# Linear attention and an MLP on one core: token groups of 864 for six of eight batches, d_ff in quarters, and a sign taken by Prelu

## The chip, the core and the metric

The kernel runs on one NeuronCore of a Trainium2 chip. The core has a matrix engine (TensorE, PE in the profile), a vector engine (VectorE, DVE), an activation engine (ScalarE, ACT), a general engine (GpSimd, POOL) and a queue engine (SyncE, SP) that starts most DMA transfers. Each works through its own list of instructions in order and waits on semaphores for the others. Matmul results land in PSUM, eight banks of 512 fp32 columns; everything else on the chip lies in SBUF. The metric is device microseconds of one launch.

## What is computed

```python
def phi(x):                                   # 8 batches, 8 heads, 576 tokens, head_dim 64; 128 features
    proj = np.einsum('bhsd,md->bhsm', x, omega)
    h = proj - np.sum(x * x, axis=-1, keepdims=True) / 2.0
    h = h - np.max(h, axis=-1, keepdims=True)
    return np.exp(h) / np.sqrt(m)
q_p, k_p = phi(q * scale), phi(k * scale)
kv = np.einsum('bhsm,bhsd->bhmd', k_p, v); z = np.sum(k_p, axis=2)
num = np.einsum('bhsm,bhmd->bhsd', q_p, kv)
den = np.einsum('bhsm,bhm->bhs', q_p, z)[..., None] + 1e-06
x = (num / den) as 4608 tokens x 512          # 8 batches x 576 tokens
h = x @ w_in                                  # 512 x 2048
g = h * erf(np.maximum(h, 0.0) + np.log1p(np.exp(-np.abs(h))))
out = g @ w_out                               # 2048 x 512
```

The weights w_in and w_out come as float64.

## The kernel before, in words

`build` records every step as an operation with the engines that may run it, an estimate of its duration on each, the tiles that it reads and writes, and for some a date (`plan`). `Plan.order` then walks through time, gives each free engine the operation with the nearest due time whose tiles have a slot, and writes one list of instructions. The engines' order is fixed by that list. `SLOTS` has the slots of each pool, `CAPS` how many of them one stream may hold.

**Attention** works in pairs of heads, four pairs (n = 4b to 4b + 3) per batch. `project` makes 128 features for 9 chunks of 128 rows in three PSUM banks (ppq, ppk), DVE takes the maxima (mxq, mxk), ACT the exponentials (fq, fk), `key_values` makes kvp, `turn` transposes the query features (pt, qh, ql), and `attend` makes numerator and denominator (nd) in two spans of 384 and 192 columns for each head (`SPANS`); ACT inverts the denominator through Ln and Exp (rc), DVE multiplies (xs). Pairs from the ninth on split their operands into a high and a low fp32r part, three matmuls for one product; the first eight run in plain fp32.

**The MoE** works batch by batch, 576 tokens as two tiles of T = 288 columns. The hidden dimension goes in two halves (`ph`), each of four d_ff tiles (`f`, 256 columns of d_ff). `split` makes high and low parts of x and of its sums (xh, xl). The first product is plain (`plain1`, banks h, eight products) for batches 0 to 2 and Winograd's form of Strassen's scheme (`gemm1`, banks hX, hY, hZ, seven products) for batches 3 to 7; each product is two contraction steps of three matmuls. `chain` takes two d_ff tiles: softplus on ACT (gs from hs), erf on ACT, the gate (hs from gs), the high part (gh) and the rest (gl). The second product (`gemm2`, blocks `e` 0 to 3 of 128 output columns, two banks o each) runs half a d_ff behind the first: `BLOCKS` sets the order f0 f1, e0, f2, e1, f3, e2, e3, where e belongs to the half before. Its banks are copied to `os` after the first half and added after the second, and stored.

**The weights** of float64 are turned into fp32 once, in 32 units of 512 KB, during batches 0 and 1: `w_load` brings the words, ACT shifts the exponent (`w_bias`), DVE shifts (`w_shift`), puts the sign in (`w_sign`) and the low word's bits (`w_tail`), then ACT makes the high part (`w_high`) and DVE the rest (`w_rest`). The finished unit is stored to DRAM (wdw) and fetched from there ever after. In batch 2 the sums for the Winograd form are made (`make_sums`, tiles R, S, cS).

What sets the order around the change: the dates of the matmuls (`at`), which start from `starts`, one entry for each half of a batch, and the dates of the pairs (`pair_time`), which spread each batch's four pairs over the batch before. Draining operations have no date of their own; theirs follows from what needs them next.

Of the kernel before, what the change touches and what calls it, by code (L numbers as in the profile page):

```python
# [329 lines left out]
def build(emit):  # L330
# [3 lines left out]
    seq = [(b, ph) for b in range(B) for ph in range(NPH)]  # L334
    starts = [START0]
    for b, ph in seq:
        starts.append(starts[-1] + FP * (STEP2 + (STEP1 if b >= PLAIN else STEP1 * 8 / 7))
                      + (NP * PAIR / 2 if b + 1 < B else 0.0))

    def begin(b):  # L340
        return starts[2 * b]

    def pair_time(n, x):
        b, p = divmod(n, NP)
        if b == 0:
# [1 line left out]
        each = (begin(b) - begin(b - 1)) / NP
        return begin(b) - LEAD - (NP - p) * each + x * each * 1.2
# [28 lines left out]
    def make(u, t):  # L377

        nm = "_".join(str(c) for c in u)
        st = pl.tile("gl", f"st{nm}", [P, HW, 2], I32, "st")  # L380
# [13 lines left out]
    def room():  # L394
        count[0] += 1
        return SLOTS["w"] - CAPS["cv"] if clock[0] < starts[2 * PLAIN + 1] else None
# [769 lines left out]
```

## Time and profile before

| | us |
|---|---|
| median of three timed runs | 1075.67 |
| their range | 1073.88 to 1076.56 |
| the profiled execution | 1073.78 |
| its span, first to last instruction | 1072.0 |

The granted TensorE clock is 0.998 of full speed over the span. The span has 21687 instructions. A row of the profile gives an engine, what it writes from what (names of tiles, buffer numbers left out), the form and the count, then busy time, the mean of one in ns, and the idle time before it with what ended it. A matmul's duration is modelled and overlaps the next one's, so a stream of matmuls is read from start to start. L824 is the line of a helper that records all of them.

### The profile page before, as it was taken

The page shows a single profiled execution, that of the slowest core. Times are in us where ns is not written, and L with a number is a line of the kernel's source. Part 1 is how long each engine was busy: PE and PEld are TensorE (multiplying, and loading weights), DVE is VectorE, ACT ScalarE, POOL GpSimd, SP SyncE. Part 2 cuts the span into 40 slices and gives each one's busy share as a digit, 9 for nine tenths or more (in the row PEclk, how much of TensorE's full clock was granted, in tenths as well). Part 3 has the DMA queues.
Part 4 walks back from the last instruction along what each step waited for, and adds up shares of the span by engine and source line. Part 5 has one row for each costly group of instructions (what it writes and reads, how often), then busy time and mean ns, then how long its engine had stood idle before and what let it go on. Part 6 is the DMA issues. An engine that isn't in the chain of part 4 may idle for free.

```text
span 1072.0 us, 21687 instructions
## 1 busy us (share of the span) xinstructions
PE 1051.2 (98%) x8272; PEld 1025.9 (96%) x8272; DVE 734.6 (69%) x1316; ACT 719.4 (67%) x1390; POOL 352.1 (33%) x306
## 2 busy tenths in 40 slices
PE   7899899999999999999999999999999999999998
PEld 7798899999999999999999999999999999999998
DVE  4889988877488586965768566766658656564431
ACT  7878878875668565867657666775667765564540
POOL 6222104100066294812334312522127222263330
PEclk9999999999999999999999999999999999999999
DMA  8376568776557777587776767768675775668771
GB/s 229 119 239 223 204 235 269 251 256 203 201 197 262 251 260 265 172 279 260 256 238 217 259 231 254 253 210 278 229 252 188 278 234 204 205 204 295 264 244 47
DMA packets 97382, 247.02 MB, mean 230 GB/s; under 512 B 10976, under 2 KB 11360, under 8 KB 97280
## 3 DMA queue, kind: packets, MB, share of 16 engines
q1 hardware_dynamic: 97216, 245.57, 67.9%
q8 instruction: 66, 1.08, 0.4%
q14 instruction: 36, 0.29, 0.1%
q0 software_dynamic: 64, 0.07, 0.0%
HBM read 210.99 MB, written 34.60 MB: 229 GB/s over the span
## 4 chain that ended last, share of the span: by engine, by line
PE 92%; DMA 3%; DVE 3%; ACT 1%; issue 1%; SPq 0%; POOL 0%; DVEq 0%; POOLq 0%; ACTq 0%
PE o L824 37%; PE h L824 13%; PE hX L824 12%; PE hY L824 6%; PE kvp L824 5%; PE nd L824 5%; PE ppq L824 4%; PE ppk L824 4%; PE hZ L824 3%; PE pt L824 2%; DMA st<-w 1%; DVE wt L824 1%; DMA uq<-qN 1%; DMA w<-wdw 1%; DVE xs L824 0%
## 5 line engine op out<-in xcount | busy, mean ns | idle before, releaser
L824 PE MATMUL o<-gh,w 128*128 128x288 f32 x2048 | 445.2, 298 | 0.2 <-ACT fq L824 0.2
L824 PEld LDWEIGHTS o<-gh,w 128*128 128x128 f32 x2048 | 339.3, 188 | 2.3 <-ACT fq L824 0.5
L824 PE MATMUL o<-gl,w 128*128 128x288 f32 x1024 | 301.7, 295 | 0.0
L824 PEld LDWEIGHTS o<-gl,w 128*128 128x128 f32 x1024 | 192.6, 188 | 0.0
L824 PE MATMUL h<-xh,w 128*128 128x288 f32 x768 | 174.6, 303 | 6.3 <-DVE w L824 2.8
L824 PE MATMUL hX<-xh,wb 128*128 128x288 f32 x640 | 162.0, 299 | 0.0
L824 PEld LDWEIGHTS h<-xh,w 128*128 128x128 f32 x768 | 129.7, 190 | 9.3 <-DVE w L824 4.5
L824 ACT ACT_TABLE_LOAD x92 | 118.0, 1283 | 2.3 <-PEq L1157 0.7
L824 PE MATMUL h<-xl,w 128*128 128x288 f32 x384 | 113.9, 297 | 0.0
L824 PEld LDWEIGHTS hX<-xh,wb 128*128 128x128 f32 x640 | 113.5, 188 | 0.4
L824 POOL TENSOR_TENSOR uk<-uk 128x288 f32<-128x288 f32 (+1 forms) x54 | 49.4, 934 | 181.4 <-DMA uk<-kN 119.9
L824 POOL TENSOR_TENSOR uq<-uq 128x288 f32<-128x288 f32 (+1 forms) x46 | 42.4, 942 | 184.5 <-DMA uq<-qN 66.1
L824 POOL TENSOR_TENSOR gl<-hs,gh 128x576 fp32r<-128x576 f32 x50 | 89.4, 1809 | 39.7 <-ACT gh L824 29.4
L824 PE MATMUL hX<-xl,wb 128*128 128x288 f32 x320 | 94.6, 296 | 0.0
L824 DVE TENSOR_REDUCE mxk<-ppk 128x4 f32<-128x512 f32 (+2 forms) x96 | 50.7, 553 | 62.1 <-PE ppk L824 61.1
L824 POOL TENSOR_TENSOR hs<-gs,hs 128x576 f32<-128x576 f32 x26 | 42.9, 1669 | 149.5 <-ACT gs L824 149.5
L824 DVE TENSOR_TENSOR hs<-gs,hs 128x1152 f32<-128x1152 f32 x51 | 81.2, 1600 | 13.4 <-ACT gs L824 13.4
L824 ACT ACTIVATE hs<-hX 128x288 f32<-128x288 f32 x75 | 30.8, 410 | 85.8 <-PE hX L824 82.9
L824 ACT ACTIVATE fq<-ppq,mxq 128x128 f32<-128x128 f32 x288 | 78.6, 386 | 13.5 <-DVE mxq L824 13.2
L824 ACT ACTIVATE rc<-nd,eps 64x192 f32<-64x192 f32 (+1 forms) x128 | 63.6, 497 | 33.3 <-PE nd L824 30.7
L824 ACT ACTIVATE fk<-ppk,mxk 128x128 f32<-128x128 f32 x288 | 79.9, 385 | 3.8 <-DVE mxk L824 3.3
L824 PE MATMUL hY<-xh,wb 128*128 128x288 f32 x320 | 81.3, 299 | 0.0
(106 smaller groups left out, 2115.9 us busy)
## 6 DMA issues: line engine op xcount, KB each, us to landing
w<-wdw SPq DMA_DIRECT2D x144, 512.0 KB, 4.9
wb<-wdcS SPq DMA_DIRECT2D x160, 256.0 KB, 4.1
wb<-wdw SPq DMA_DIRECT2D x120, 256.0 KB, 3.9
st<-w SPq DMA_DIRECT2D x32, 512.0 KB, 5.1
wdw<-w SPq DMA_DIRECT2D x32, 512.0 KB, 3.7
v<-vP SPq DMA_DIRECT2D x32, 325.0 KB, 4.3
out<-os SPq DMA_DIRECT2D x32, 288.0 KB, 3.6
wdcS<-cS SPq DMA_DIRECT2D x16, 512.0 KB, 5.1
```

The costliest lines, as they stand in the source:

```text
L824: return tc.keep_in_program_order(method(*args, **kwargs))
```

## The change

**Token groups.** `SUPERS` puts groups in place of batches: two of 2 x 288 tokens and four of 2 x 432. Groups 0 to 2 are plain, 3 to 5 Winograd. `FROM` has where each begins, `pieces` maps a span of a batch to the tiles of the groups, `need` has the last batch that a group needs: 0, 1, 3, 4, 6, 7. So the pairs of two batches fall into group 1's time and into group 3's. The sums for the Winograd form are made in group 2 (`SUMS`).

**Quarters.** d_ff goes in four parts of two tiles (`NQ`, `GP`). In each the two tiles' products are merged, then come the four blocks e of the part before. Each block takes one unit of w_out and 24 matmuls. Its two banks are copied to `os` in the first part and added in the other three.

**Pools.** hs, gs, gh, gl and what attention borrows from them share one pool "g" of ten slots; staging, R and S share the pool "w" with the weights. Blocks o may hold three PSUM banks in place of two.

**Dates.** Drains of h, hX, hY, hZ and o are due `DRAIN` = 2 us behind their last matmul, the divisions get a date from `DIVIDE`, and the planner's estimates of matmuls, drains and DMA issues follow the tile's width.

**Smaller parts.** `SPANS` becomes 288 and 288. ACT's `w_bias` is a Prelu whose slope gives negative numbers their sign bit, and `w_sign` goes. The maxima of the pairs from the ninth on stay in the middle PSUM bank until they are shifted. Omega is loaded from ACT's queue in place of POOL's. The output is one array of 512 x 4608. `less` and `exponential_all` are not used, since `LESS` is empty.

```diff
-T = 288
+SUPERS = ((288, True), (288, True), (432, True), (432, False), (432, False), (432, False))
+FROM = tuple(2 * sum(t for t, _ in SUPERS[:i]) for i in range(len(SUPERS) + 1))
+SUMS = max(i for i, (_, plain) in enumerate(SUPERS) if plain)
+NG = NPH * FP
+GP = 2
+NQ = NG // GP
...
-SLOTS = dict(w=8, u=3, f=2, mx=3, sq=3, v=2, qh=1, ql=1, kh=1, kl=1, xs=4, xh=2, xl=2,
-             hs=4, gs=2, gh=6, gl=6, os=4, ps=8)
-CAPS = dict(st=2, wt=2, wp=2, cv=2, att=4, moe1=5, moe2=2)
+SLOTS = dict(w=8, g=10, u=2, f=2, mx=3, sq=3, v=2, qh=1, ql=1, kh=1, kl=1, xs=10, xh=2, xl=2,
+             os=4, ps=8)
+CAPS = dict(st=2, wt=1, wp=2, cv=2, att=4, moe1=5, moe2=3, hs=4, gs=2, w=6)
...
-SPANS = ((0, 384), (384, 192))
-BLOCKS = ((("f", 0), ("f", 1)), (("e", 0),), (("f", 2),), (("e", 1),), (("f", 3),), (("e", 2),), (("e", 3),))
+SPANS = ((0, 288), (288, 288))
+DRAIN = 2.0
+DIVIDE = 4.0
...
+    need = [max(b for b in range(B) if FROM[i] < (b + 1) * S and b * S < FROM[i + 1])
+            for i in range(len(SUPERS))]
+    step = [3 * mm(t) * (8 if plain else 7) * KH for t, plain in SUPERS]
+    per = [NG * step[i] + NQ * KT * 2 * GP * 2 * 3 * mm(SUPERS[i][0]) for i in range(len(SUPERS))]
+    more = [(need[i + 1] - need[i]) * NP if i + 1 < len(SUPERS) else 0 for i in range(len(SUPERS))]
...
-        pl.op("psign", [("V", 0.68, -1e9)], lambda e: E.w_sign(st, w), reads=[(st, 0), (w, 0)],
-              writes=[(w, 0)])
...
-            pl.op("hout", [("A", 0.42, -1e9), ("V", 0.46, 0.0)],
-                  lambda e: E.h_out(e, hs.ap[:, i, t, :], hp), reads=[(hp, 0)], writes=[(hs, (i, t))])
+            pl.op("hout", [("A", d["A"], -1e9), ("V", d["V"], 0.0)],
+                  lambda e: E.h_out(e, hs.ap[:, i, t, :], hp, T), reads=[(hp, 0)], writes=[(hs, (i, t))],
+                  plan=clock[0] + DRAIN)
...
+            for block in (("f", 0), ("e", 0), ("e", 1), ("e", 2), ("e", 3)):
+                what, x = block
                 if what == "f":
-                    lists.append((plain1 if b < PLAIN else gemm1)(b, ph, x))
+                    gs = range(GP * q, GP * q + GP)
+                    merged([(plain1 if plain else gemm1)(b, *divmod(g, FP)) for g in gs])
+                    chain(b, gs)
                 elif last:
-                    lists.append(gemm2(*last, x))
+                    merged([gemm2(*last, x)])
...
-    pool.dma_start(om[D:P], omT)
-    pool.dma_start(om[0:D], omT)
+    act.dma_start(om[D:P], omT)
+    act.dma_start(om[0:D], omT)
...
         def w_bias(self, e, t, w):
-            dst, src = w.ap.bitcast(F32), t.ap[:, :, 1].bitcast(F32)
-            if e == "A":
-                act.activation(dst, src, AF.Copy, scale=2.0 ** -112)
...
+            act.activation(w.ap.bitcast(F32), t.ap[:, :, 1].bitcast(F32), AF.Prelu, scale=2.0 ** -112,
+                           alpha=-2.0 ** 32)
...
-        def shift(self, mx, sq):
-            for x in (-half_sq, half_sq):
-                dve.scalar_tensor_tensor(mx.ap, sq.ap, x, mx.ap, op0=ALU.mult, op1=ALU.add)
+        def shift(self, mx, raw, sq):
+            for dst, x in ((raw, -half_sq), (mx.ap, half_sq)):
+                dve.scalar_tensor_tensor(dst, sq.ap, x, raw, op0=ALU.mult, op1=ALU.add)
```

On DVE, while batch 0's first product runs, unit 5 of w_in is unpacked; wt1_0_5 is its PSUM tile, w1_0_5 the finished unit. Before:

```order
L824 TENSOR_SCALAR wt1_0_5_775<-wt1_0_5_775 128x512
L824 SCALAR_TENSOR_TENSOR wt1_0_5_775<-st1_0_5_716,wt1_0_5_775 128x512
L824 TENSOR_REDUCE mxk_1_1_746<-ppk_1_1_2_791 128x3
L824 COPY qh_1_0_812<-pt_1_0_1_800 128x384
L824 COPY qh_1_0_812<-pt_1_0_2_808 128x384
L824 SCALAR_TENSOR_TENSOR wt1_0_5_775<-st1_0_5_716,wt1_0_5_775 128x512
L824 TENSOR_SCALAR wt1_0_6_828<-wt1_0_6_828 128x512
L824 TENSOR_TENSOR w1_0_5_6_717<-wt1_0_5_775,w1_0_5_6_717 128x2x256
```

and now:

```order
L874 TENSOR_SCALAR wt1_0_5_776<-wt1_0_5_776 128x512
L874 SCALAR_TENSOR_TENSOR wt1_0_5_776<-st1_0_5_706,wt1_0_5_776 128x512
L874 TENSOR_REDUCE mxk_1_1_745<-ppk_1_1_2_788 128x3
L874 COPY hs0_0_1_739<-h010_0_1_750 128x288
L874 COPY qh_1_0_807<-pt_1_0_2_810 128x384
L874 TENSOR_TENSOR w1_0_5_6_707<-wt1_0_5_776,w1_0_5_6_707 128x2x256
```

One of two operations from st to wt is gone, and the unit's last step stands one operation nearer.

On DVE in group 1 (batch 1 before), around a pair of batch 2 (its first before, its second now); os0_0 is block 0 of group 0's output, xs the pair's result. Before:

```order
L824 COPY hs1_0_0_2229<-h111_0_0_2318 128x288
L824 TENSOR_TENSOR w2_1_0_1_30_2201<-wt2_1_0_1_2312,w2_1_0_1_30_2201 128x2x256
L824 TENSOR_TENSOR xs_2_0_2388<-nd_2_0_0_0_2291,rc_2_0_0_2341 64x384
L824 TENSOR_TENSOR xs_2_0_2388<-nd_2_0_1_0_2324,rc_2_0_0_2341 64x384
L824 TENSOR_TENSOR xs_2_0_2388<-nd_2_0_0_1_2330,rc_2_0_1_2373 64x192
L824 TENSOR_TENSOR xs_2_0_2388<-nd_2_0_1_1_2337,rc_2_0_1_2373 64x192
```

and now:

```order
L874 TENSOR_TENSOR os0_0_1258<-o0_3_0_0_2619,os0_0_1258 128x288
L874 TENSOR_SCALAR wt2_1_2_1_2580<-wt2_1_2_1_2580 128x512
L874 SCALAR_TENSOR_TENSOR wt2_1_2_1_2580<-st2_1_2_1_2506,wt2_1_2_1_2580 128x512
L874 TENSOR_TENSOR w2_1_1_1_34_2418<-wt2_1_1_1_2488,w2_1_1_1_34_2418 128x2x256
L874 TENSOR_TENSOR xs2_1_0_2711<-nd_2_1_0_0_2663,rc_2_1_0_2680 64x288
L874 TENSOR_TENSOR xs2_1_0_2711<-nd_2_1_1_0_2686,rc_2_1_0_2680 64x288
L874 TENSOR_TENSOR os0_0_1258<-o0_3_0_1_2646,os0_0_1258 128x288
L874 TENSOR_TENSOR xs2_1_0_2711<-nd_2_1_0_1_2694,rc_2_1_1_2708 64x144
L874 TENSOR_TENSOR xs2_1_0_2711<-nd_2_1_1_1_2700,rc_2_1_1_2708 64x144
L874 TENSOR_TENSOR xs2_1_1_2744<-nd_2_1_0_1_2694,rc_2_1_1_2708 64x144
L874 TENSOR_TENSOR xs2_1_1_2744<-nd_2_1_1_1_2700,rc_2_1_1_2708 64x144
```

Group 0's last part of d_ff (o0_3) is added there, the last units of w_out (w2_1_2_1) are unpacked, and the pair's second span falls into two tiles of group 2 in four operations for two.

On PE at the end, where the last part of d_ff goes through the second product; gh and gl are a d_ff tile's high and low part. Before, the first half's block 3 ends and the second half's block 0 begins, o7_1_0:

```order
L824 MATMUL o7_0_3_1_12881<-gh7_0_3_12425,w2_0_3_1_328_12768 128x288
L824 MATMUL o7_1_0_0_12946<-gh7_1_0_12677,w2_1_0_0_329_12783 128x288
L824 MATMUL o7_1_0_0_12946<-gl7_1_0_12697,w2_1_0_0_329_12783 128x288
L824 MATMUL o7_1_0_0_12946<-gh7_1_0_12677,w2_1_0_0_329_12783 128x288 x2
L824 MATMUL o7_1_0_0_12946<-gl7_1_0_12697,w2_1_0_0_329_12783 128x288
L824 MATMUL o7_1_0_0_12946<-gh7_1_0_12677,w2_1_0_0_329_12783 128x288
```

and now the third part's block 3 ends and the fourth part's begins, o5_3:

```order
L874 MATMUL o5_2_3_1_11126<-gh5_5_10871,w2_1_3_0_236_11012 128x432
L874 MATMUL o5_3_0_0_11149<-gh5_6_11100,w2_1_0_1_237_11049 128x432
L874 MATMUL o5_3_0_0_11149<-gl5_6_11113,w2_1_0_1_237_11049 128x432
L874 MATMUL o5_3_0_0_11149<-gh5_6_11100,w2_1_0_1_237_11049 128x432 x2
L874 MATMUL o5_3_0_0_11149<-gl5_6_11113,w2_1_0_1_237_11049 128x432
L874 MATMUL o5_3_0_0_11149<-gh5_6_11100,w2_1_0_1_237_11049 128x432
L874 MATMUL o5_3_0_1_11159<-gh5_6_11100,w2_1_0_1_237_11049 128x432
```

Each matmul has half as many columns again, and the last part needs two d_ff tiles where the last half needed four; three banks (o5_3_0_0, o5_3_0_1, o5_3_1_0) take tile 6 before tile 7 is called for.

More of the change, by code (lines that the diff above doesn't have):

```diff
@@ L333, in build, with mm, pieces @@
     E = emit
[L334 to L341 removed]
+    def mm(n):
+        return 0.012 + n / 2400
+    def pieces(b, c0, w):
+        out, a, end = [], b * S + c0, b * S + c0 + w
+        while a < end:
+            i = max(x for x in range(len(SUPERS)) if FROM[x] <= a)
+            t = SUPERS[i][0]
+            h, o = divmod(a - FROM[i], t)
+            n = min(end - a, t - o)
+            out.append((i, h, o, a - b * S - c0, n))
+            a += n
+        return out
+    first = [pieces(b, 0, 1)[0][0] for b in range(B)]
+    last_ = [pieces(b, S - 1, 1)[0][0] for b in range(B)]
+    need = [max(b for b in range(B) if FROM[i] < (b + 1) * S and b * S < FROM[i + 1])
[3 more added lines that the diff above has]
+    more = [(need[i + 1] - need[i]) * NP if i + 1 < len(SUPERS) else 0 for i in range(len(SUPERS))]
+    starts = [START0]
+    for i in range(len(SUPERS)):
+        starts.append(starts[-1] + per[i] + more[i] * PAIR)
     def pair_time(n, x):
         b, p = divmod(n, NP)
[L345 removed]
+        if b <= need[0]:
             return n * FIRST + x * 14.0
[L347 to L348 removed]
+        i = next(i for i in range(len(SUPERS)) if need[i] >= b)
+        each = (starts[i] - starts[i - 1]) / more[i - 1]
+        k = (need[i] + 1) * NP - n
+        return starts[i] - LEAD - k * each + x * min(each, 33.0) * 1.2
     xh, xl = {}, {}
@@ L395, in room @@
         count[0] += 1
[L396 removed]
+        return CAPS["w"] if clock[0] < starts[SUMS + 1] else SLOTS["w"]
     def unit(u):
@@ new lines, in split, with half, flat @@
+    def split(b, c):
+        T, plain = SUPERS[b]
+        n = 4 if plain else len(XB)
+        h = xh[b, c] = pl.tile("xh", f"xh{b}_{c}", [P, n, T], F32R)
+        l = xl[b, c] = pl.tile("xl", f"xl{b}_{c}", [P, n, T], F32R)
+        def half(p, t):
+            x, keys = xs[b, p, t]
+            return lambda: x.ap, [(x, k) for k in keys]
+        b11, b12, b21, b22 = half(c, 0), half(c, 1), half(c + KH, 0), half(c + KH, 1)
+        def flat(x):
+            return lambda: x().rearrange("p (a t) -> p a t", a=1)
+        parts = [(i, 1, flat(x[0]), x[1]) for i, x in enumerate((b21, b22, b11, b12)[:4 if plain else 3])]
+        if not plain:
+            xc = pl.tile("g", f"xc{b}_{c}", [P, 4, T], F32, "xc", 1)
@@ L753, in one @@
+            if f == n - 1:
                 out(t)
-                if ph and t:
+                if q == NQ - 1 and t:
                     pl.op("ostore", [("S", 0.1, 1e9)], lambda e: E.o_store(o, b, et), reads=[(o, 0), (o, 1)],
-                          plan=clock[0] + 3.0, size=P * S * 4)
-        return [lambda h=h, t=t, fi=fi: one(h, t, fi) for h in range(2) for t in range(2)
-                for fi in range(FT // 2)]
+                          plan=clock[0] + 3.0, size=P * 2 * T * 4)
+        return [lambda t=t, f=f: one(t, f) for t in range(2) for f in range(n)]
```

263 lines of the change are left out of this document (137 added, 126 removed).

## The prediction

> **What bounds the kernel now.** I read the page first, then the busy times by stage, then the chain of waits at the end, then single groups. The page's head, its busy line and its chain by engine:
>
> ```profile
> span 1072.0 us, 21687 instructions
> PE 1051.2 (98%) x8272; PEld 1025.9 (96%) x8272; DVE 734.6 (69%) x1316; ACT 719.4 (67%) x1390; POOL 352.1 (33%) x306
> PE 92%; DMA 3%; DVE 3%; ACT 1%; issue 1%; SPq 0%; POOL 0%; DVEq 0%; POOLq 0%; ACTq 0%
> ```
>
> TensorE (PE) is the bound nearly everywhere. Where it isn't shows when the span is cut into stages. Below, the columns are the stretch, its length, then busy us with instruction counts for PE, weight loads, DVE, ACT and POOL, then clock, DMA share and GB/s. Rows one to three end where the first softplus of batch 0, 1 and 2 starts on ACT (the two rows of the second fence are the first two such starts); the fourth is batch 5; the fifth the last batch; the sixth is one slice out of batch 0's stage.
>
> ```profile
> 0.00:79.20 79.20, 69.76 (x504) 63.90 (x504) 58.87 (x117) 63.14 (x172) 31.67 (x37) 1.00 0.65 193
> 79.20:200.10 120.90, 113.63 (x851) 107.61 (x851) 106.19 (x176) 99.33 (x194) 23.14 (x25) 0.99 0.67 233
> 200.10:332.70 132.60, 132.60 (x1071) 130.48 (x1070) 98.21 (x172) 92.14 (x177) 30.55 (x33) 1.00 0.66 229
> 590.70:717.10 126.40, 126.40 (x1024) 124.13 (x1024) 86.79 (x165) 87.52 (x167) 39.13 (x34) 1.00 0.73 244
> 961.10:1072.00 110.90, 107.05 (x809) 106.82 (x807) 34.88 (x54) 42.84 (x51) 26.71 (x16) 1.00 0.63 213
> 80.40:107.20 26.80, 24.50 (x170) 23.43 (x170) 24.92 (x40) 24.10 (x38) 5.70 (x4) 0.94 0.65 223
> ```
> ```profile
> 79.25 1.17 ACT L824 ACTIVATE gs<-hs 128x1152 f32<-128x1152 f32 x1
> ...
> 200.06 1.16 ACT L824 ACTIVATE gs<-hs 128x1152 f32<-128x1152 f32 x1
> ```
>
> From 200 us on PE never rests. Before that it does: in batch 0's stage DVE and ACT are as full as they get (24.92 of 26.80 us, 93%, in the slice), since the weights are unpacked there. So there are two kinds of time to change: the length of PE's stream, and its gaps before 200 us.
>
> **PE's stream: matmuls of 432 columns for 288.** The stream at the end is nothing but o matmuls, and a pair of batch 2 or later shows 384 and 192 columns in a row (start, modelled duration, name):
>
> ```profile
> 1030.78 37.39 PE o L824 x282
> ...
> 553.27 0.34 PE L824 MATMUL nd<-qh,kh 128*128 128x384 f32 x1
> 553.44 0.33 PE L824 MATMUL nd<-ql,kh 128*128 128x384 f32 x1
> 553.62 0.33 PE L824 MATMUL nd<-qh,kl 128*128 128x384 f32 x1
> 553.78 0.25 PE L824 MATMUL nd<-qh,kh 128*128 128x192 f32 x1
> ...
> 554.43 0.32 PE L824 MATMUL hX<-xh,wb 128*128 128x288 f32 x1
> ```
>
> 37.39 / 282 = 0.1326 us from one 288-column matmul to the next. Three of 384 columns take 553.78 - 553.27 = 0.51 to 0.52, 0.173 each. No row has 432 columns. The line through the two points rises (0.173 - 0.1326) / 96 = 0.42 ns per column and gives 0.173 + 48 x 0.42 ns = 0.1932 us. The bounds: a cost in columns alone gives 1.5 x 0.1326 = 0.1989; a matmul that hides its fixed part entirely at 432 gives 432 x 0.42 ns = 0.181. I take 0.1932, the line from the nearest row.
>
> Counts come from the program. Before, the MoE has 384 matmuls per batch for the second product and 384 (three plain batches) or 336 (five Winograd batches) for the first: 8 x 384 + 3 x 384 + 5 x 336 = 5904, x 0.1326 = 782.9 us. After, two groups of 288-tiles make 2 x 768 = 1536; one plain and three Winograd groups of 432-tiles make 768 + 3 x 720 = 2928. The plain part grew from 1728 to 2016 tokens, so the columns grow too, by 2928 x 432 + 1536 x 288 - 5904 x 288 = 6912. Time: 1536 x 0.1326 + 2928 x 0.1932 = 203.7 + 565.7 = 769.4, **13.5 us less**. With 0.1989 it is 786.1, 3.2 more; with 0.181 it is 733.7, 49 less.
>
> The Trainium skill's TensorE: Matmul & The Clock Gate, section "Back-to-back issue gap", gives N / 2.4 + 2.5 ns per warm matmul: 122.5 ns at 288 columns and 182.5 at 432. By that the sum would be 723.2 before and 722.5 after, an estimate from the page: 1440 fewer fixed parts are eaten by 6912 more columns. The trace has 132.6 ns at 288, so here the part that isn't columns is larger than the page's, and the row decides.
>
> Attention's nd blocks go from 384 + 192 to 288 + 288 columns. Before, six of 384 and six of 192 for a pair: 6 x 0.173 + (554.43 - 553.78) = 1.69; after, 12 x 0.1326 = 1.59. For 24 such pairs **2.4 less**. If the 192s get cheaper neighbours, nothing; at most 24 x 0.2 = 5. The first eight pairs run whole fp32 matmuls with the same columns: nothing.
>
> **The weights' unpacking.** Who PE waited for from 79 to 200 us, and the groups on DVE and ACT that change (busy, mean ns, idle before):
>
> ```profile
> PE h L824 <- DVE w L824: 2.8, 3, 1.6
> PE h L824 <- ACT w L824: 1.6, 1, 1.6
> ```
> ```profile
> L824 DVE SCALAR_TENSOR_TENSOR wt<-st,wt 128x512 int32<-128x512 int32 x64 | 44.4, 693 | 1.4
> L824 DVE TENSOR_TENSOR xs<-nd,rc 64x384 f32<-64x384 f32 x64 | 35.3, 551 | 5.4 <-ACT rc L824 4.4
> L824 DVE TENSOR_TENSOR os<-o,os 128x288 f32<-128x288 f32 x64 | 29.0, 454 | 51.2 <-PE o L824 51.0
> L824 DVE TENSOR_TENSOR xs<-nd,rc 64x192 f32<-64x192 f32 x64 | 22.6, 353 | 4.4 <-ACT rc L824 2.5
> L824 DVE SCALAR_TENSOR_TENSOR mxq<-sq,mxq 128x9 f32<-128x9 f32 x48 | 19.2, 400 | 1.6
> L824 DVE SCALAR_TENSOR_TENSOR mxk<-sk,mxk 128x9 f32<-128x9 f32 x48 | 10.6, 222 | 1.5
> L824 ACT ACTIVATE wt<-st 128x512 f32<-128x512 f32 x32 | 20.2, 637 | 4.2 <-DMA st<-w 4.0
> L824 ACT ACTIVATE w<-wt 128x512 fp32r<-128x512 f32 x32 | 19.0, 597 | 4.7 <-DVE wt L824 4.6
> ```
>
> Prelu in place of Copy lets 32 of the 64 wt operations go: 32 x 0.693 = 22 us of DVE's time. But quarters of d_ff bring work back. Every unit of both weights is now called for by the time group 0's last quarter goes through the second product, one quarter behind the first; before, the second half of w_out came half a d_ff behind, well into batch 1. By the program's order, DVE starts 24 units between the first gate of group 0 and that of group 1, against 17; it drains 26 o banks there against 4 (22 x 0.454 = 10 us); 24 xs operations stand there for 16; and attention is half a pair further. All of DVE's operations of this stretch, each with its row's mean, sum to 118 us before, where the trace shows 106.19 busy (neighbours overlap), and to 144 after; scaled alike, 130. At the 93% of the fullest slice that takes 140 us. PE gets more done in it: 96 o matmuls (12.7 us) and half a pair (3), so the stage would be 120.9 + 15.7 = 136.6 with gaps unchanged. I book **+4**; DVE at the 88% of the stage row (106.19 of 120.90) would take 148, +12; no gap at all by DVE's list would give 130, -7.
>
> Group 1 then carries two batches of attention, since group 2 needs batches 2 and 3. PE's content: 384 o and 288 h of 288 columns, 96 h of 432, seven pairs. A pair is (132.60 - 768 x 0.1326) / 4 = 7.7 us by the plain stage, less the 0.1 above: 89.1 + 18.5 + 53.2 = 161. DVE's list there sums to 158 by the same reckoning against 106 for batch 1 (98.21 busy): 146 busy, 91% of 161. Batch 1 ran at 74% without a gap, batch 0 at 88% with gaps. I book **+4**, between 0 and 146 / 0.8 = 182, +21. Later groups are safe: group 3, again with two batches, has DVE at 73% of its PE time, as batch 5 (86.79 of 126.40).
>
> Before 79 us five units' worth of unpacking on DVE is lighter by some 6.6 us, on a stage where chains of one engine after the other decide: **-2**, between 0 and -6.
>
> Prelu itself and the maximum kept in a PSUM bank have no row. The two activations of 512 elements take 0.64 and 0.60 us; I take 0.64 for Prelu, 0.1 either way, 3 us of ACT over 200: nothing. The shifted maximum (0.222 to 0.400 each, 96 of them) may move by 0.15 either way, 14 us of DVE over 860 us, beside PE: nothing.
>
> **Ends.** The load of omega moves from POOL's queue to ACT's, behind its table load:
>
> ```profile
> 0.74 1.28 ACT L824 ACT_TABLE_LOAD   x1 [0.74 <-PEq L1157]
> 1.27 1.23 POOL L824 DMA_DIRECT2D om<-omT  x2 [0.82 <-POOLq L1157]
> 3.87 0.22 DVE L824 TENSOR_SCALAR wk<-om 64x128 f32<-64x128 f32 x1 [2.61 <-DMA om<-omT]
> 4.20 4.18 PE L824 MATMUL ppk<-wk,uk 128*128 128x128 f32 x18 [4.20 <-DVE wk L824]
> ```
>
> If the issue waits for the table it starts at 2.02 for 1.27, and PE starts 0.75 later, behind it the squares on ACT; if not, 0.5 earlier. **+0.5.** At the far end, the last two d_ff tiles go through softplus, erf, gate and split before the last o matmuls:
>
> ```profile
> 1030.82 0.41 ACT L824 ACTIVATE hs<-hX 128x288 f32<-128x288 f32 x1 [3.55 <-PE hX L824]
> 1036.07 2.22 ACT L824 ACTIVATE gs<-gs 128x1152 f32<-128x1152 f32 x2
> 1039.93 2.60 DVE L824 TENSOR_TENSOR gl<-hs,gh 128x1152 fp32r<-128x1152 f32 x1 [1.30 <-ACT gh L824]
> 1042.60 2.82 POOL L824 TENSOR_TENSOR gl<-hs,gh 128x576 fp32r<-128x576 f32 x2 [1.28 <-ACT gh L824]
> 1068.26 0.46 DVE L824 TENSOR_TENSOR os<-o,os 128x288 f32<-128x288 f32 x1 [0.40 <-PE o L824]
> ```
> ```profile
> out<-os SPq DMA_DIRECT2D x32, 288.0 KB, 3.6
> ```
>
> The chain took 1045.42 - 1030.82 = 14.6 us; its first tile's parts were ready at 1042.53. Half as many elements again (the two table loads aside) make some 16 for the first tile and 20 for the second. After the last hX, 93 o matmuls of the third part (18.0) and 18 on the first tile (3.5) stand ahead, 21.5. So **nothing**, with 1.5 to spare; if a step slips by more than that, each us counts. The last drain (0.46) and store (3.6, most of it no matter of size) are half as large again: **+0.6**, between 0.2 and 2.
>
> **The sum.** -13.5 - 2.4 + 4 + 4 - 2 + 0.5 + 0.6 = -8.8. The profiled execution took 1073.78 us, 1.78 more than its span, which gives 1065.0. It lies 1.89 under the median of the three timed runs, 1075.67, which gives 1066.8. I write **1066**.
>
> **Rivals.** (a) DVE and ACT hold the first two groups: batch 0's stage comes at +12 and group 1 at +21 instead of 4 and 4, as PSUM banks and pairs wait behind 17 us more of sums and 7 units more of unpacking. That gives 1066 + 25 = 1091, and is slower than before from a joint surcharge of about 21 us on. For it: 91% of DVE in group 1, and PE waits for w in the rows above. Against: PE has banks of both products to go to. Middle price 1084; chance 0.17. (b) A matmul's cost lies nearly in its columns: at 0.196 to 0.199 the stream gains 5 or loses 3, and the time is 1074 to 1082. The single gaps between 384s, 0.17 to 0.18 in the rows above, don't exclude 0.196. Chance 0.14, mostly no change. (c) The gaps of the first group close by half, because the shorter chain (ACT, DVE, DVE, ACT, DVE) feeds PE in time and drains are dated. Batch 0's stage holds 576 MoE matmuls (76.4) and four pairs at 5.8 to 7.7, 99 to 107 us of PE's work in 120.9, so 14 to 21 of gaps: -9 in place of +4, and 0 in place of +4, make 1049. For it: PE waited for w; against: DVE's list is longer. Chance 0.17. (d) The change doesn't reach the end: the last chain exceeds its cover by 5 or more and a wait on a bank recurs in each e block: 1072, no change. Chance 0.05. The forecast has 0.47.
>
> **How the numbers follow.** A difference of 0.3%, 3.2 us, is about what a measurement of this kernel can tell. The forecast, 1058 to 1074, holds faster 0.39, same 0.07, slower 0.01; (a) same 0.03, slower 0.14; (b) faster 0.02, same 0.09, slower 0.03; (c) faster 0.17; (d) same 0.05. Together faster 0.58, same 0.24, slower 0.18. The range runs from 1048, the middle of (c), to 1084, that of (a); half of each lies outside.
>
> **What would show it.** 432-column matmuls 0.193 us apart in the last stretch, against 0.196 or more. First softplus of group 1 some 140 us after that of group 0, and of group 2 some 165 after that. PE without idle time from there to its end, no wait for gl at the last part. If PE waits in group 2 to 5, for o or h banks or for w, my sum lacks a term. Wrong altogether would be a stage after group 1 that takes longer than its matmul count.

## The result, and the profile after

The changed kernel takes 1066.03 us (median of four runs, 1063.53 to 1066.12), the kernel before beside it 1075.97. The ratio is 0.9907, 95% interval [0.989, 0.9924]: 0.9% faster. The profiled execution took 1066.02, 1.8 more than its span. The head of its page, its busy line and its chain by engine:

```profile
span 1064.2 us, 18256 instructions
PE 1045.1 (98%) x6832; PEld 992.5 (93%) x6832; DVE 726.4 (68%) x1258; ACT 679.1 (64%) x1299; POOL 378.2 (36%) x288
PE 93%; DVE 3%; DMA 2%; ACT 1%; issue 1%; SPq 0%; ACTq 0%
```

1440 matmuls fewer, and PE is the bound as before, busy 6.1 us less. Cut again where the first softplus of each group starts (columns as before: stretch, length, busy us and instructions of PE, weight loads, DVE, ACT and POOL, clock, DMA share, GB/s):

```profile
0.00:82.40 82.40, 73.09 (x527) 67.68 (x528) 56.51 (x117) 63.74 (x174) 30.84 (x38) 0.98 0.62 184
82.40:223.60 141.20, 135.76 (x1036) 130.49 (x1034) 123.41 (x220) 116.60 (x229) 20.70 (x24) 0.98 0.70 245
223.60:379.90 156.30, 156.30 (x1252) 151.38 (x1251) 120.22 (x239) 109.69 (x242) 44.97 (x50) 1.00 0.60 204
379.90:558.70 178.80, 178.56 (x1110) 167.90 (x1110) 125.23 (x208) 112.87 (x202) 93.50 (x62) 1.00 0.55 184
558.70:756.90 198.20, 198.20 (x1273) 186.14 (x1272) 146.44 (x265) 121.86 (x254) 88.79 (x63) 1.00 0.57 186
756.90:919.00 162.10, 162.10 (x928) 154.03 (x927) 99.02 (x150) 91.99 (x145) 69.86 (x37) 1.00 0.50 163
919.00:1064.20 145.20, 141.12 (x720) 134.85 (x718) 55.53 (x63) 62.37 (x59) 29.50 (x14) 1.00 0.47 157
```

The first groups are where the two engines are full (DVE 123.41 of 141.20, 87%), and they cost PE only 141.20 - 135.76 = 5.4 us of rest; group 1 has none. What PE waited for in that second stretch (us in all, times, longest), and the last 189 matmuls of the stream with an earlier run of 93, from the chain of waits:

```profile
PE o L874 <- DVE w L874: 2.1, 3, 0.8
PE h L874 <- ACT w L874: 1.3, 1, 1.3
PE o L874 <- ACT w L874: 1.0, 1, 1.0
PE h L874 <- DVE w L874: 0.6, 1, 0.6
```
```profile
987.68 18.24 PE o L874 x93
1022.95 37.18 PE o L874 x189
```

These are 5.0 of the 5.4 us, and all of them are for an unpacked weight. And 37.18 / 189 = 0.1967 us from one 432-column matmul to the next (18.24 / 93 = 0.1961 in the earlier run), not the 0.1932 of the forecast.

**A ledger for reading the runs.** Three numbers of each profiled execution split its span. Idle is the span less PE's busy time (the busy line). Clock loss is one less the mean granted clock, times the span. Work is the rest, the busy time as it would be at full clock. Before: 1072.0 - 1051.2 = 20.8 idle, clock 0.998, so 2.1 of loss, 1049.1 of work. After: 19.1 idle, clock 0.995 and 5.3 of loss, 1039.8 of work. So **work fell by 9.3, idle by 1.7, and the clock took back 3.2**. The clock has three digits, so each loss is good to half a us, and busy times are modelled. But kernels with the same matmuls ought to show the same work, and below those of the changed kernel do within 2.4 us, but for e11, which is 4.6 above it. The medians below leave out one execution, of e7, which took 2536.92 us.

### The profile page after: what moved, and what is told of

It reads as the page before. It is cut to its first block, busy times and chain, and to the rows that moved or that the text cites. A ratio compares the mean times of both kernels' runs of the same rounds, so it can differ in the third digit from the quotient of the medians.

```text
span 1064.2 us, 18256 instructions
## 1 busy us (share of the span) xinstructions
PE 1045.1 (98%) x6832; PEld 992.5 (93%) x6832; DVE 726.4 (68%) x1258; ACT 679.1 (64%) x1299; POOL 378.2 (36%) x288
## 4 chain that ended last, share of the span: by engine, by line
PE 93%; DVE 3%; DMA 2%; ACT 1%; issue 1%; SPq 0%; ACTq 0%
PE o L874 36%; PE h L874 16%; PE hX L874 11%; PE kvp L874 5%; PE hY L874 5%; PE nd L874 5%; PE ppq L874 4%; PE ppk L874 4%; PE hZ L874 3%; PE pt L874 2%; DMA st<-w 1%; DVE wt L874 1%; DVE w L874 0%; ACT L874 0%; DVE os L874 0%
## 5 line engine op out<-in xcount | busy, mean ns | idle before, releaser
L874 PE MATMUL o<-gh,w 128*128 128x432 f32 (+1 forms) x1536 | 412.0, 341 | 3.4 <-DVE w L874 2.1
L874 PE MATMUL o<-gl,w 128*128 128x432 f32 (+1 forms) x768 | 259.6, 338 | 0.0
L874 PE MATMUL h<-xh,w 128*128 128x288 f32 (+1 forms) x768 | 197.6, 327 | 1.8 <-ACT w L874 1.3
L874 POOL TENSOR_TENSOR hs<-gs,hs 128x864 f32<-128x864 f32 x32 | 80.3, 2533 | 172.4 <-ACT gs L874 172.4
L874 DVE TENSOR_TENSOR os<-o,os 128x432 f32<-128x432 f32 (+1 forms) x144 | 78.6, 552 | 82.1 <-PE o L874 81.7
L874 PE MATMUL hX<-xh,wb 128*128 128x432 f32 x384 | 123.8, 364 | 0.0
L874 PE MATMUL h<-xl,w 128*128 128x288 f32 (+1 forms) x384 | 122.0, 318 | 0.0
L874 POOL TENSOR_TENSOR gl<-hs,gh 128x864 fp32r<-128x864 f32 x40 | 85.6, 2163 | 14.3 <-ACT gh L874 9.5
L874 PEld LDWEIGHTS h<-xl,w 128*128 128x128 f32 x384 | 73.1, 190 | 1.3
L874 DVE TENSOR_TENSOR xs<-nd,rc 64x288 f32<-64x288 f32 (+1 forms) x160 | 62.9, 393 | 14.9 <-ACT rc L874 11.7
L874 PE MATMUL kvp<-v,fk 128*128 128x65 f32 (+1 forms) x576 | 68.4, 272 | 1.2 <-PE ppq L874 0.8
```

What stands on the lines that cost most here:

```text
L874: return tc.keep_in_program_order(method(*args, **kwargs))
```

## The experiments

The medians stand beside 1075.0 to 1075.7 for the kernel before, run in the same four sittings, each on another chip; the column of ratios is against that. The other columns are of the one profiled execution; "to group 2" is the start of group 2's first softplus, so the opening and groups 0 and 1 together.

| run | median us | ratio, interval | span | to group 2 | idle | clock loss | work |
|---|---|---|---|---|---|---|---|
| before | | | 1072.0 | | 20.8 | 2.1 | 1049.1 |
| after | 1066.03 | 0.9907 [0.989, 0.9924] | 1064.2 | 379.9 | 19.1 | 5.3 | 1039.8 |
| e1 all tiles 288 | 1077.69 | 1.0027 [1.0014, 1.004] | 1076.1 | | 23.0 | 5.4 | 1047.7 |
| e2 sign back | 1077.62 | 1.0018 [1.0008, 1.0029] | 1073.5 | 387.7 | 26.1 | 7.5 | 1039.9 |
| e3 before with Prelu | 1077.69 | 1.0023 [1.0015, 1.0032] | 1077.7 | | 23.1 | 5.4 | 1049.2 |
| e4 spans back | 1078.46 | 1.0046 [1.0029, 1.0063] | 1075.7 | 388.9 | 26.4 | 5.4 | 1043.9 |
| e5 sign, same list | 1073.96 | 0.999 [0.9974, 1.0005] | 1069.4 | 385.1 | 23.9 | 4.3 | 1041.2 |
| e6 room for the sign | 1075.84 | 1.0012 [0.9993, 1.0031] | 1070.9 | 385.1 | 26.7 | 5.4 | 1038.8 |
| e7 LEAD 29 | 1076.5 | 1.0019 [1.0002, 1.0036] | 1070.5 | 385.7 | 26.3 | 4.3 | 1039.9 |
| e8 PAIR 8.7 | 1073.25 | 0.9982 [0.9966, 0.9998] | 1072.5 | 387.0 | 26.6 | 5.4 | 1040.5 |
| e9 unchanged | 1063.54 | 0.989 [0.9872, 0.9908] | 1061.2 | 376.8 | 19.0 | 2.1 | 1040.1 |
| e10 two plain groups | 1076.75 | 1.0 [0.9983, 1.0017] | 1073.3 | 401.4 | 31.7 | 12.9 | 1028.7 |
| e11 no dates | 1099.5 | 1.0219 [1.0204, 1.0235] | 1097.7 | 401.8 | 40.1 | 13.2 | 1044.4 |
| e12 dates in before | 1069.74 | 0.9951 [0.9933, 0.9969] | 1067.9 | | 19.8 | 0.0 | 1048.1 |

### e1: all tiles of 288

```diff
-SUPERS = ((288, True), (288, True), (432, True), (432, False), (432, False), (432, False))
+SUPERS = ((288, True), (288, True), (288, True)) + ((288, False),) * 5
```

> The changed kernel with SUPERS of eight groups of 2 x 288 tokens (three plain, five Winograd), so quarters, pools, dates and Prelu stay and only the token groups go back to batches. Theory A (PE's stream: fewer, longer matmuls): the MoE has 5904 matmuls of 288 columns again, 5904 x 0.1326 = 782.9 us against 203.7 + 2928 x 0.196 = 777.6 with the 0.196 us that the changed kernel's trace shows, so 5 us slower than the changed kernel, 1071, less whatever group 1 gains when it carries one batch of attention instead of two. Theory B (the gain is the unpacking's, the width of the tiles gives nothing): 1066 or a few us less.

1077.69, 11.7 above the changed kernel and above both theories. The ledger puts 7.9 of the 11.9 us of span down to work and 3.9 to idle. At 0.1967 us a matmul the wide tiles take 203.7 + 2928 x 0.1967 = 779.6 us and the width is worth 782.9 - 779.6 = 3.3 us; by the ledger it is up to 7.9. It can't be read more finely: against before, which differs from e1 in width by nothing and in spans by the 4 us of e4, e1's work is only 1.4 less. Where the other 2.7 went stays open.

### e2: the sign back on VectorE

```diff
+        pl.op("psign", [("V", 0.68, -1e9)], lambda e: E.w_sign(st, w), reads=[(st, 0), (w, 0)],
+              writes=[(w, 0)])
-            act.activation(w.ap.bitcast(F32), t.ap[:, :, 1].bitcast(F32), AF.Prelu, scale=2.0 ** -112,
-                           alpha=-2.0 ** 32)
+            act.activation(w.ap.bitcast(F32), t.ap[:, :, 1].bitcast(F32), AF.Copy, scale=2.0 ** -112)
```

> The changed kernel with Copy and w_sign in place of Prelu, so 32 x 0.69 = 22 us more on DVE, 24 units of it (16.6 us) between the first softplus of group 0 and that of group 1. Theory A (that stage is held by DVE's list, 141 us long at 92% busy): the stage grows by 16.6 / 0.92 = 18 us and the opening by 2 or 3, 1086. Rival (DVE's time is hidden beside PE, chains decide): within 4 us of 1066.

1077.62, 11.6 more: between the two. Idle is up by 7.0, work is the same. The stretches of groups 0 and 1:

```profile
78.50:220.10 141.60, 131.97 (x976) 126.67 (x975) 125.78 (x216) 106.70 (x212) 23.20 (x29) 0.95 0.64 223
220.10:387.70 167.60, 165.10 (x1316) 159.11 (x1317) 131.47 (x265) 113.71 (x256) 46.63 (x50) 1.00 0.62 211
```

Group 1's stage is 11.3 longer (167.60 for 156.30) and group 0's, which holds most of the unpacking, only 0.4. Yet of the added idle time 4.2 us lie in group 0 (141.60 - 131.97 = 9.6 for 5.4) and 2.5 in group 1: some 60 of PE's matmuls have moved from the one stage to the other. So the whole order had changed, and the lengths of single stages don't tell where an edit costs.

### e3: Prelu alone, in the kernel before

```diff
-        pl.op("psign", [("V", 0.68, -1e9)], lambda e: E.w_sign(st, w), reads=[(st, 0), (w, 0)],
-              writes=[(w, 0)])
-            act.activation(w.ap.bitcast(F32), t.ap[:, :, 1].bitcast(F32), AF.Copy, scale=2.0 ** -112)
+            act.activation(w.ap.bitcast(F32), t.ap[:, :, 1].bitcast(F32), AF.Prelu, scale=2.0 ** -112,
+                           alpha=-2.0 ** 32)
```

> The kernel before with Prelu in place of Copy and w_sign, nothing else changed. Theory A: batch 0's stage (120.9 us, DVE 88% busy) loses 17 x 0.69 = 11.8 us of DVE's list and has 14 to 21 us of gaps, so 8 to 12 us faster than before, about 1066: as much as the whole change. Rival (chains of waits decide there, not DVE's list): within 4 us of 1076.

1077.69, if anything slower. In its page the group of 64 operations wt<-st,wt on DVE is one of 32, 22.2 us busy for 44.4; idle rose by 2.3 all the same, and the clock took 3.3. Relief of the engine that looks fullest brought nothing here. But the planner, told of it, wrote another order in this run too, so what the relief is worth in an order that stays is not shown by it; e5 asks that of the changed kernel.

### e4: attention's spans back to 384 and 192

```diff
-SPANS = ((0, 288), (288, 288))
+SPANS = ((0, 384), (384, 192))
```

> The changed kernel with SPANS of 384 and 192 columns again. Theory A: 24 pairs x 0.1 to 0.18 us of nd matmuls come back, 2 to 4 us slower, 1068 to 1070. Rival (the nd matmuls' length is lost in waits of the pairs): no difference.

1078.46, 12.4 more, where 2 to 4 were expected. 4.1 of it is work, which is the edit; 7.3 is idle, which the edit doesn't explain. It sits elsewhere than in e2: 4.8 of it in the opening (84.50 - 70.37 = 14.1 for 9.3) and 3.9 in group 1, whose stage takes 170.1.

### e5 and e6: the sign's cost apart from the order

Three edits of quite different kinds (e1, e2, e4) had each cost some 12 us, and in each the planner had written another order: in e2, some 600 of TensorE's 1920 planned operations stand at another place of its list than in the changed kernel. So the two were separated: e5 adds the operations to an order that isn't touched, e6 changes the order and adds nothing.

e5, with Copy for Prelu as in e2:

```diff
         def w_tail(self, t, w):
+            dve.scalar_tensor_tensor(w.ap, t.ap[:, :, 1], -2 ** 31, w.ap,
+                                     op0=ALU.bitwise_and, op1=ALU.bitwise_or)
```

e6:

```diff
-        pl.op("ptail", [("V", 0.68, -1e9)], lambda e: E.w_tail(st, w), reads=[(st, 0), (w, 0)],
+        pl.op("ptail", [("V", 1.36, -1e9)], lambda e: E.w_tail(st, w), reads=[(st, 0), (w, 0)],
```

> The changed kernel with the sign taken back to an operation of VectorE (Copy on ScalarE, 32 scalar_tensor_tensor more on VectorE), but the planner is not told of it: every list of every engine is that of the changed kernel, with the 32 operations put in just ahead of the tails. e2 put the sign back with the planner told, which reshuffled the lists, and came 11.6 us above the changed kernel. Theory D (VectorE's time in the first two groups is what counts): the 32 x 0.69 = 22 us cost the same half as in e2, so 1077 +- 2, with the second group's stage at 167 us as in e2. Theory L (the lists count, the operations hardly): 1066 to 1069, first two stages within 3 us of 141 and 156.

> The mirror image: Prelu stays and no instruction is added, but the planner books the tail of each unit at twice its cost (1.36 for 0.68), as if the sign still stood there, so the lists are reshuffled much as in e2. Theory D: no VectorE work is added, so 1066 +- 2. Theory L: the list is another one and the time moves by several us, most likely up, towards 1072 to 1078.

The stretches of groups 0 and 1, of e5 and then of e6 (columns as above):

```profile
80.70:228.50 147.80, 136.81 (x1032) 129.89 (x1031) 137.52 (x243) 113.56 (x227) 20.63 (x24) 0.98 0.67 235
228.50:385.10 156.60, 156.60 (x1255) 151.68 (x1254) 121.24 (x240) 109.68 (x242) 45.03 (x50) 1.00 0.60 204
```
```profile
80.70:227.10 146.40, 136.03 (x1040) 130.13 (x1038) 120.52 (x211) 120.06 (x238) 21.60 (x27) 0.98 0.68 232
227.10:385.10 158.00, 157.98 (x1262) 152.92 (x1262) 122.77 (x248) 105.11 (x235) 45.82 (x51) 1.00 0.61 208
```

Both theories hold in part. With the order kept, 14 us more of DVE (137.52 for 123.41) make the stage 6.6 longer, 5.6 of it idle: DVE is now 93% full there, the fullness of the prediction's slice. With no work added, another order gives 4.9 more of idle in the same stage, with DVE at 82%. So Prelu is worth about 5 us of gaps in this order, and an order alone is worth as much.

### e7 and e8: neutral edits

```diff
-LEAD = 30.0
+LEAD = 29.0
```
```diff
-PAIR = 8.6
+PAIR = 8.7
```

> The changed kernel with LEAD 29.0 for 30.0: the pairs of batch 2 and later are planned 1 us later; nothing is added or removed, but about 1570 of 5280 rows of TensorE's list and 490 of VectorE's 1260 stand elsewhere. Theory D: 1066 +- 2. Theory L: a draw from a spread of some +-6 us; over 4 us from 1066 in this run or the next speaks for L.

> The changed kernel with PAIR 8.7 for 8.6: the starts of groups 1 to 5 are planned up to 0.4 to 2 us later; nothing is added or removed, about 1210 rows of TensorE's list and 435 of VectorE's stand elsewhere. Theory D: 1066 +- 2. Theory L: another draw, over 4 us from 1066 in this run or the last; the difference sits in the stages before the first softplus of group 2 (82, 141 and 156 us in the changed kernel), and stages 179, 198, 162 and 145 behind it stay within 2 us.

1076.5 and 1073.25, 10 and 7 above the changed kernel, for planned dates that move by a us or two. Work is the same within 0.7; idle is up by 7.2 and 7.5, all of it ahead of group 2 but 1 to 2 us. Here e7's stretch of groups 0 and 1:

```profile
77.90:215.40 137.50, 128.43 (x980) 122.74 (x978) 113.60 (x203) 107.44 (x206) 25.23 (x31) 0.99 0.65 226
215.40:385.70 170.30, 166.53 (x1318) 160.79 (x1319) 132.56 (x267) 113.68 (x250) 47.42 (x53) 0.99 0.61 207
```

Its PE idles 9.1 us in group 0 for the changed kernel's 5.4, and 3.8 in group 1, where the changed kernel doesn't stand at all. The median of e7 lies above its profiled execution (1072.32, clock 0.996). The other executions have no profile, but the clock of each is on record: 0.995 to 0.997 in the three others under 1075, 0.990 to 0.993 in the seven from 1076.0 to 1080.2. By the ledger, 0.003 to 0.006 less clock is 3 to 6 us of the 4 to 8 between them.

### e9: the changed kernel again

> The changed kernel itself, not a line different, beside the others and on their chip: the 1066.03 us were four runs on another chip, and six variants of it have come out at 1073 to 1078 with before at 1075. Theory L (its list is a good draw): again 1064 to 1068, 9 below before. Theory C (the chip or the day makes the difference): 1070 to 1075, and then what e2 and e4 to e8 lost against it is smaller than it looked.

1063.54, ratio 0.989. The result repeats. e9 ran beside e10 and e11, on another chip than e2 and e4 to e8; but as the kernel before took 1075.0 to 1075.7 in every sitting, the chips differ by less than 1 us, and the 7 to 12 us between the changed kernel and its neighbours are the neighbours' own.

### e10: only two plain groups

```diff
-SUPERS = ((288, True), (288, True), (432, True), (432, False), (432, False), (432, False))
+SUPERS = ((288, True), (288, True), (432, False), (432, False), (432, False), (432, False))
```

> Group 2 in Winograd form, so that only the two 288-groups are plain: 48 matmuls of 432 columns less, 48 x 0.196 = 9.4 us of TensorE's stream. The sums of the weights' quarters, and the stores of the four sums of each pair of units, move from group 2 to group 1, where VectorE is already the fullest but one. Theory D: the stage of group 1 grows by 5 to 15 (156 to 161-171), that of group 2 shrinks by 9 (179 to 170): 1062 to 1072. If VectorE's work in group 1 were covered: 1057. Theory L: the same mean of 1066 - 9 + 7 for another draw, and the stage of group 2 at 170 in any case.

1076.75, above what both theories said. Work fell by 11.1, the 9.4 of 48 matmuls and a little more, and 20 us of idle and clock took its place. Groups 0 to 2, and PE's longest wait:

```profile
80.30:214.60 134.30, 128.49 (x972) 123.39 (x971) 116.09 (x202) 108.83 (x208) 32.91 (x36) 0.97 0.67 237
214.60:401.40 186.80, 173.56 (x1344) 166.28 (x1346) 147.56 (x291) 127.75 (x279) 74.74 (x75) 0.95 0.67 227
401.40:567.90 166.50, 166.50 (x1037) 157.02 (x1035) 113.70 (x193) 101.20 (x182) 71.24 (x46) 1.00 0.59 194
```
```profile
PE o L874 <- ACT w L874: 7.3, 2, 6.3
```

Group 2 shrinks as expected, 178.8 to 166.5. Group 1 has the sums now and grows by 30.5 us where 5 to 15 were expected: DVE does 147.56 for 120.22, PE waits 6.3 us in one piece for a weight across the stage's start, idles 13.2 in all and runs at 0.95 of its clock, 9 us more. How much of this is the sums and how much another order is not separated.

### e11 and e12: the dates for emptying PSUM

e11, at each of the five drains of h and o:

```diff
-                  plan=clock[0] + DRAIN)
+                  plan=None)
```

e12, in the kernel before at the same five, of which one is shown:

```diff
-                  lambda e: E.h_out(e, hs.ap[:, i, t, :], hp), reads=[(hp, 0)], writes=[(hs, (i, t))])
+                  lambda e: E.h_out(e, hs.ap[:, i, t, :], hp), reads=[(hp, 0)], writes=[(hs, (i, t))],
+                  plan=clock[0] + DRAIN)
```

> The changed kernel without the dates for emptying PSUM (the drains of h and o get their due time from what follows them, as before the change); the work is the same. If the dates are what keeps banks free in the first two groups: PE waits more for o and h banks there, 1072 to 1085, with more idle time ahead of o<-DVE or h<-ACT than the 4.4 us of the changed kernel. If they do nothing: 1066 as a list of the same kind, or some 1072 to 1076 as another draw.

> The kernel before the change with one part of the change alone: the drains of h and o get a due time, 2.0 us behind the planner's clock, as in the changed kernel; tiles of 288, halves of d_ff, the sign and the spans stay. Taking the dates out of the changed kernel (e11) cost 36 us, 25 of them before group 2 and 7.6 in group 4. Theory G (the dates by themselves give the gain, and the tiles little): 1055 to 1066, with the stage of batch 0 at 105 to 113 for 120.9. Theory N (they only make up for what the other parts of the change bring: quarters of d_ff, 26 drains for 4 in the first group and longer drains; where there are 4 drains, a date has nothing to hurry): 1071 to 1078, and the later stages, at 126 us without any wait of TensorE, don't move in either case.

e11 is the largest effect of the study, 1099.5. Its stretches of groups 0 and 4, then e12's of batches 0 and 1:

```profile
79.80:239.60 159.80, 144.72 (x1022) 134.55 (x1022) 129.05 (x230) 119.51 (x227) 17.61 (x20) 0.94 0.62 217
...
782.80:952.40 169.60, 165.01 (x934) 155.83 (x933) 104.69 (x156) 91.31 (x142) 64.01 (x34) 0.99 0.48 159
```
```profile
79.80:194.70 114.90, 110.09 (x843) 105.47 (x842) 108.53 (x181) 95.66 (x184) 23.01 (x25) 1.00 0.70 245
194.70:330.10 135.40, 134.82 (x1083) 132.15 (x1083) 97.80 (x173) 91.61 (x178) 34.95 (x35) 1.00 0.65 225
```

Group 0 has 15.1 us of idle for 5.4, at clock 0.94. Group 4, where DVE and ACT have room, gets 4.6 of idle for none, and both its waits are for a bank that is being emptied:

```profile
PE o L874 <- DVE os L874: 3.6, 1, 3.6
PE hX L874 <- ACT hs L874: 1.0, 1, 1.0
```

In group 0 the longest waits are not the expected ones for o and h banks but others, for attention's steps:

```profile
PE nd L874 <- ACT fk L874: 4.2, 7, 1.0
PE pt L874 <- DVE ql L874: 3.0, 2, 2.6
```

A drain's only followers in the planner's graph are what reads its result, often far off; the bank that it frees is not in its due time, so without a date it can be put off while a matmul is short of a bank. The waits of group 4 show that. In group 0, how the missing dates lead to the waits is not shown. In all it is 21 us of idle in the changed kernel, 8 of clock and 4.6 that the ledger calls work, though the matmuls are the same; 7 of the idle, as in e6 to e8, may be no more than another order. In the kernel before, the date gives 5.2 us (0.9951), about half way between the two theories: batch 0's stage is 6.0 shorter, batch 1's 2.8 longer, and the later ones stay at 126 as both said. Of the 4.1 us between the two profiled spans 1.0 is idle, 2.1 clock and 1.0 work. But the clock is not what the date gained: executions with a recorded clock of 1.000 took 1067.83, 1069.15 and 1069.74 with the dates, and 1073.70 and 1074.17 without them in the same sitting. Where those 5 us lie, the two profiles don't show. Nor is it shown how much of the change's 9 us the dates give in the changed kernel, where their absence costs more than the whole change gains.

## Why the prediction came out right

The total is right, and two of its largest terms are wrong against each other: work fell by 6.6 us less than forecast, idle and clock rose by 5.6 less. That they cancel is luck, and so is the order: with those of e6 and e7 the same work takes 1075.84 and 1076.5, outside the forecast's 1058 to 1074.

- **The matmuls' pitch, the term of -13.5: mis-sized.** The step that failed is the line through 0.1326 at 288 and 0.173 at 384. It rested on one run of three matmuls, and 3.5 ns on 0.193 make 10 us over 2928 matmuls. The same trace had more: start to start, neighbouring 384-column matmuls have a median of 174 to 175 ns, from which the same line gives 195 to 196. At 0.1967 the prediction's own sum is 203.7 + 575.9 = 779.6, **3.3** less than before (5.0 with the 0.1961 of the earlier run). That is the pitch of rival (b), though not its time, since the gaps that were booked did not come. From e4, the work beside the spans fell by 9.3 - 4.1 = **5.2**, on a ledger that scatters by some 2 us. The slope is (196.7 - 132.6) / 144 = 0.445 ns for a column for 0.42, and the part that isn't columns only 132.6 - 288 x 0.445 = 4.4 ns. The Trainium skill's rule that the prediction weighed (TensorE: Matmul & The Clock Gate, "Back-to-back issue gap"), which the section gives for a single matmul on its own, would have 182.5 ns; the measurement decides against it, though the estimate by it for both kernels, 0.7 less, was nearer than mine.
- **The spans, -2.4: a little small.** e4 shows 4.1 of work, inside the 5 allowed.
- **Batch 0's stage, +4 and 140 us: the stage right, the reason not.** It took 141.2. But the booked +4 was for gaps, and they shrank, 7.3 to 5.4 us; PE was busy 22.1 us longer in the stage, where 15.7 were counted, some 1.7 of it for one more stretch at half the clock. Rival (c) reckoned with 14 to 21 us of gaps in this stage before; the prediction's own row has 120.90 - 113.63 = 7.3.
- **Group 1, +4 and 165 us: wrong.** 156.3, without any idle. DVE is at 77% of it where 91% was reckoned, so the list that I summed overstated its load (146 us busy for 120.22), and PE's own content was put at 161.
- **Are the surcharges a wrong rule, then?** For this order, yes. For its neighbours e6 to e8 idle is 7.2 to 7.6 higher, about the 8 that were booked. Sums of DVE's work by stage give what such a kernel costs in a typical order; they don't see which order the planner found. That was the doubt left out, in both directions.
- **The opening, -2 + 0.5: wrong in the first.** 82.4 us for 79.2, and 80.3 in e9; idle 9.3 for 9.4, so lighter unpacking shortened no chain, and in e3's opening the idle is 10.7. PE is busy 3.3 us longer there (73.09 for 69.76). Omega's load was on the other branch, 0.37 earlier. Its rows:

```profile
0.73 1.28 ACT L874 ACT_TABLE_LOAD   x1 [0.73 <-PEq L1211]
0.76 1.46 ACTq L874 DMA_DIRECT2D om<-omT  x2
3.83 4.21 PE L874 MATMUL ppk<-wk,uk 128*128 128x128 f32 x18 [3.83 <-ACT uk L874]
```

  The issue did not wait for the table, and PE now waits for the squares.
- **The end, 0 and +0.6: right.** The last 189 o matmuls are one unbroken piece, so the chain of the last tiles stayed within its cover; from its end to the span's end are 4.07 us for 3.83, so 0.24 where 0.6 was booked.
- **No gaps from group 2 on: right**, 0.2 us in groups 2 to 4, and in group 5 none ahead of the last matmul. Neither rival (a) nor (d) occurred. Rival (c) was right on group 1, which has no gap, and had the drains' dates among its reasons: without them (e11) the kernel is where (a) said or beyond, though another order may have a part in that.

So: work -9.3 for the forecast's -15.9; idle and clock +1.5 for its +7.1, together -7.8 for -8.8.

## What to carry to other kernels

Where a planner writes the order, any edit draws a new one, and here that alone was worth 7 us of gaps and some clock besides: run a neutral edit or two, and split the span into work, idle and clock, before a difference of that size is put down to the edit. A pitch that is to be multiplied by thousands wants a long run of the same shape. And an operation that frees a bank needs a due time of its own, since what waits for the bank isn't among its followers.

## What the hardware showed besides

A short gap can halve TensorE's clock, and the same gap need not. The changed kernel and e9 are the same program. Ahead of the same o matmuls, both waited 1.0 us for ACT and 0.6 for DVE, some 1.7 of idle. First the changed kernel's stretches of one us, then e9's:

```profile
114.00:115.00 1.00, 0.58 (x6) 0.33 (x4) 1.00 (x2) 1.00 (x6) 0.00 (x0) 1.00 0.93 373
115.00:116.00 1.00, 0.38 (x2) 0.30 (x2) 1.00 (x3) 1.00 (x4) 0.00 (x0) 1.00 0.66 128
116.00:117.00 1.00, 0.37 (x3) 0.22 (x2) 1.00 (x3) 1.00 (x6) 0.00 (x0) 1.00 0.91 328
117.00:118.00 1.00, 1.00 (x9) 1.00 (x8) 1.00 (x2) 1.00 (x3) 0.00 (x0) 0.85 0.95 375
118.00:119.00 1.00, 1.00 (x7) 0.99 (x6) 1.00 (x2) 1.00 (x4) 0.26 (x1) 0.50 1.02 410
119.00:120.00 1.00, 1.00 (x6) 1.00 (x5) 0.69 (x3) 0.10 (x1) 1.00 (x2) 0.50 1.07 397
120.00:121.00 1.00, 1.00 (x6) 1.00 (x5) 0.97 (x2) 0.20 (x1) 0.03 (x1) 0.50 0.92 234
121.00:122.00 1.00, 1.00 (x9) 1.00 (x8) 0.86 (x2) 1.00 (x5) 0.00 (x0) 0.94 0.90 356
```
```profile
112.00:113.00 1.00, 0.76 (x7) 0.52 (x6) 1.00 (x2) 1.00 (x5) 0.00 (x0) 1.00 0.92 352
113.00:114.00 1.00, 0.19 (x1) 0.19 (x2) 1.00 (x3) 1.00 (x4) 0.00 (x0) 1.00 0.75 192
114.00:115.00 1.00, 0.38 (x3) 0.14 (x2) 1.00 (x3) 1.00 (x5) 0.00 (x0) 1.00 0.83 272
115.00:116.00 1.00, 1.00 (x8) 1.00 (x9) 1.00 (x2) 1.00 (x4) 0.00 (x0) 1.00 0.91 356
116.00:117.00 1.00, 1.00 (x10) 1.00 (x9) 1.00 (x2) 1.00 (x4) 0.10 (x1) 1.00 1.02 413
```

In the first the clock is at 0.50 for some 3.4 us, a loss of 0.15 + 3 x 0.50 + 0.06 = 1.7 us; in the second it stays at 1.00. The Trainium skill's TensorE: Matmul & The Clock Gate, section "Part 1: The HAM clock gate", says that the clock is either full or half and is judged over a free-running window of about 3.4 us; the half and its length agree here. The same page's "HAM oscillation" asks for no gap over some 3.4 us; here gaps of at most 1.0, 1.7 in sum, were enough.

Why only one of two equal gaps is hit can be read from the traces, which keep the moment of each change of the clock. In all fourteen profiled executions every stretch at half the clock ahead of the last matmul lasts 3.413 us or two or three times that, and within an execution they begin whole multiples of 3.413 us apart. Cut by that grid, the 1.7 us of idle in the changed kernel fall into one window, 114.29 to 117.71, in which PE is busy 1.75 us; in e9 the edge of a window, at 113.96, parts them, and PE is busy 2.34 us in the window before it and 2.80 in the one behind. The others agree: each of the 36 drops of the clock follows a window with PE busy for at most 0.65 of it; at full clock, every window with 0.48 or less is followed by a drop, and between 0.49 and 0.65 (by modelled busy times) it goes either way.

So a gap's price is its own length and, where it takes about half of one such window, 1.7 us more, and the executions of one kernel differ by such steps: of the 3.0 us between the spans of the changed kernel and e9, the ledger puts 3.2 down to the clock.
